# A planned one-core attention and gated-product kernel: two accumulating transfers more per query block, four more up tiles through ScalarE, four batches of value head sums, and nine wide dummy matmuls

## The chip, the cores and the metric

The kernel runs on one core of one Trainium2 chip. The metric is device microseconds of one execution. The kernel before was run three times: 265.95, 266.19 and 266.68 us, median 266.19 us. One more execution, of 266.25 us, was profiled, and the rows quoted in this document are of that one. The engines are called as in the profile: PE (TensorE matmuls), PEld (its weight loads), DVE (VectorE), ACT (ScalarE), POOL (GpSimd) and SP (the engine that issues most transfers).

## The reference

The input x has 2048 rows of 640 columns. Everything is bfloat16 at the ends.

```python
xn = _layernorm(x)
qkv = xn @ wqkv                     # 32 heads of 20, q, k, v
idx = pos[:, None] - 2 * arange(8)  # eight keys per row, two apart, none before row 0
logits = einsum("bhsd,bhswd->bhsw", q, k[idx]) * 20 ** -0.5
o = einsum("bhsw,bhswd->bhsd", softmax(logits), v[idx])
h = (xn' @ w_gate) * (xn' @ w_up)   # 1536 columns
return x + o @ wo + h @ w_down
```

Here xn' is the same normalised x. So there are three kinds of work: dense products with weights (q, k, v, gate, up, down, wo), the eight shifted products of q and k with their head sums, and the eight weighted sums over v.

## The kernel before

**Planner.** The kernel is written as tasks with the tiles that they read and write. A class `Sched` (lines 50 to 351) picks, task by task, the one that could start first on its engine by a table of costs that stands in the code (`occ`, `lat`, and for accumulating transfers `acc` in lines 149 to 153), and writes out one fixed instruction order for each engine with the waits between them. So the costs are used only while the program is written; on the chip each engine runs its list in order, and each instruction waits for what it needs. A change of a cost can reorder everything behind it.

**Tiling.** The 2048 rows are four blocks j of 512. The transposed normalised x is `XNT`; the 640 columns are five chunks c of 128, and the 1536 columns of gate and up are twelve tiles m of 128. PSUM has eight banks of 512 columns.

**Dense work on PE.** `proj_group`, `proj_v` and `q_bank` make q, k and v (lines 698 and 730). `gu` (line 1287) goes through pairs (j, m) in the order of `SEQ` (line 1277): five matmuls of 512 columns with a gate tile, then five with an up tile (line 1314). ACT copies the gate result out of PSUM (line 703). The up result is multiplied in by DVE straight from PSUM (line 1323), unless the pair is in `FAST` (line 1467): then ACT copies the up tile too, into one of two tiles `UF` (`fev`, line 1357), and DVE multiplies two bfloat16 tiles (line 1361). `dn` and `dn_piece` (lines 1387 and 1400) add up twelve matmuls with w_down and five with wo for each piece of 128 rows and 320 columns (line 1416); for blocks 0 to 2 the result leaves through ACT into `FB0` and an accumulating transfer `oadd` into the output (line 1442).

**Logits.** For blocks 0 and 1 DVE makes products of q and k for four shifts at once (`narrow`, line 880), and PE adds up heads with a matrix of ones (line 1012). For blocks 2 and 3 chunks 0 to 3 are made by `wide`, two shifts at once, in fp32, straight from the PSUM bank of q (line 929, tiles `PRF`), and are added on POOL before PE sees them. For each block, each half r of the shifts and each pair of shifts q0 there are four chunk products and one product of the fifth chunk, so four additions:

- `sum32` with p = 0 adds chunk 1 to chunk 0 (name `qsum{j}_{r}_{q0}_0`); for (r, q0) in `BY_DMA[0]` by an accumulating transfer in SBUF that POOL issues (line 951), else by a POOL add (line 955);
- the same call then adds the fifth chunk (name with `c` at its end, line 966; line 962 if (r, q0) is in `LAST_DMA`, which is empty);
- `close` calls `sum32` with p = 1, again by transfer or by add;
- `qend{j}_{r}_{q0}` is the last add, always on POOL (line 988).

Blocks 2 and 3 are joined: PE sums their heads (line 1012) in one group of sixteen matmuls when all eight `qend` are done. PE's list is in order, so it stands still there if they are late. Softmax of blocks 2 and 3 comes behind it.

**Values.** `weighted` and `unit` (lines 1134 and 1151) take twenty units u, five for each block: DVE multiplies v by the weights (line 1191) into one of three tiles `PV`, POOL adds the two halves (line 1196) into `SV`, two adds for each unit, and PE sums heads with four small matmuls for each unit (line 1250) in batches that end with the units in `BATCH` (line 1105): five, five, five, three and two units. Each unit of a batch needs a PSUM bank; ACT copies it out into `OT` (line 1259), which the wo matmuls read.

**Start.** `warm(18)` (line 1495) makes PE multiply zeros before any input has landed.

Of the kernel before, what the change touches and what calls it, by code (L numbers as in the profile page):

```python
# [15 lines left out]
NF = 12  # L16
# [5 lines left out]
TS = 128  # L22
JB = 512
HB = 1024
QB = 256
# [24 lines left out]
class Sched:  # L50
# [78 lines left out]
    def op(self, eng, fn, r=(), w=(), dma=False, name="", occ=None, lat=None, lock=False, nbytes=0, mode=0, group=None, extra=0.0, acc=0.0, land=None):  # L129
        X = _Op()  # L130
        X.eng, X.fn, X.name, X.dma, X.group = eng, fn, name, dma, group
        X.needs_tick, X.event, X.pre_know, X.idx = False, None, None, len(self.ops)
        X.nth = self.n_eng[eng]
        self.n_eng[eng] += 1
        rk = [k for a in r for k in self.keys(a)]
        wk = [k for a in w for k in self.keys(a)]
        deps = self.deps_of(eng, rk, wk)
        if lock:
            deps.update({d.idx: d for d in self.port["pool" if eng == "dve" else "dve"]})
        if occ is None and not dma:  # L140
            occ = 0.1
        inorder = eng in ("pe", "act", "dve")
        start = max([self.t[eng]] + [d.end for d in deps.values()])
        if lock:
            start = max(start, self.t_lock)
        if eng == "pe" and mode != self.pe_mode:
            start += 0.1
            self.pe_mode = mode
        if dma:
            self.t[eng] = start + (0.48 if occ is None else occ)  # L150
            if acc:
                self.t_acc = max(self.t_acc, start + 3.8) + acc
                X.end = self.t_acc
            else:
                self.t_data = max(self.t_data, start + 1.2) + nbytes / 280e3
                X.end = self.t_data + 0.8 + extra
            if land is not None:
                X.end, self.t_data = land, max(land - 0.8, self.t_data - nbytes / 280e3)
        else:
            self.t[eng] = start + occ  # L160
            X.end = start + (occ if lat is None else lat)
        if lock:
            self.t_lock = start + occ
        last = {}
        keep = []
        for d in deps.values():
            if d.dma or d.eng == "pool":
                keep.append(d)
            else:
                b = last.get(d.eng)  # L170
                if b is None or b.idx < d.idx:
                    last[d.eng] = d
        X.deps = keep + list(last.values())
        for d in X.deps:
            if not d.dma:
                d.needs_tick = True
        for k in rk:
            st = self.state.get(k)
            if st is None:
                self.state[k] = [None, [X]]  # L180
            elif inorder and st[1] and st[1][-1].eng == eng and not st[1][-1].dma:
                st[1][-1] = X
            else:
                st[1].append(X)
        for k in wk:
            self.state[k] = [X, []]
        if dma:
            if group is None or group not in self.groups:
                sem = self.nc.alloc_semaphore(f"dma{self.n_dma}")
                self.n_dma += 1  # L190
                if group is not None:
                    self.groups[group] = [sem, []]
            if group is None:
                X.event = (sem, 16)
            else:
                g = self.groups[group]
                g[1].append(X)
                X.event = (g[0], 16)
        if lock:
            self.port[eng] = [X] if eng == "dve" else self.port[eng] + [X]  # L200
            if eng == "dve":
                self.port["pool"] = []
        self.ops.append(X)
        return X
# [151 lines left out]
def build_kernel(nc, A_x, A_wqkv, A_wo, B_x, B_w_gate, B_w_up, B_w_down, out):  # L356
    K = Sched(nc)
    op = K.op
# [63 lines left out]
    PRD += [sb("PRD12", [128, 4, JB], at=a_sc), sb("PRD13", [128, 4, JB], at=a_sc + 4096)]  # L422
    PRD32 = [K.sbuf(f"PRF{i}", [128, 2, JB], FP32, K.base[p.name]) for i, p in enumerate(PRD)]
    QUAD = {2: (1, 0), 3: (1, 0)}
    LAST_DMA = ()
    BY_DMA = (((0, 0), (0, 2)), ((1, 0), (1, 2)))
    a_xr = place[0]
    FB0 = sb("FB0", [128, 5, D])
# [12 lines left out]
    ZERO = sb("ZERO", [128, JB])  # L441
# [235 lines left out]
            yield Task("sp", dmat, r=[xs], prio=1)  # L677
        mark("xnt", t)

    def warm(n):  # L680
        for _ in range(n):
            op("pe", lambda e: e.matmul(PS[:, 7, 0:QB], ZERO[:, 0:128], ZERO[:, 0:QB], start=True, stop=True),
               r=[ZERO[:]], w=[PS[:, 7, :]], name="warm", occ=0.2 if n > 3 else 0.12)

    def wcols(which, c, m):
        if which == 2:
# [77 lines left out]
    def proj_qk():  # L764
        for pair in (0, 2):
            for which in (0, 1):
                for t in (pair, pair + 1):
                    yield have("xnt", t)
                    K.spawn(proj_group([(which, 0, 4 if pair else 5)], t * TS, TS, 10 if pair else FIRST + 0.5 * which + 0.2 * t, None))
            if pair:  # L770
                for which in (0, 1):
                    K.spawn(proj_group([(which, 4, 1)], pair * TS, 2 * TS, 10.2, None))
        for t in (4, 6):
            yield have("xnt", t + 1)
            for items in ([(0, 0, 2)], [(1, 0, 2)], [(0, 2, 2)], [(1, 2, 2)], [(0, 4, 1), (1, 4, 1)]):
                K.spawn(proj_group(items, t * TS, 2 * TS, 11 + t * 0.1, None))
        for j in (2, 3):
            yield have("xnt", 4 * j + 3)
            for m in range(NCH):
                for which in (0, 1):  # L780
                    if which or j not in QUAD or m == NCH - 1:
                        K.spawn(proj_group([(which, m, 1)], j * JB, JB, 12 + j, None))
# [61 lines left out]

    def products():
        rows = {j: [] for j in range(NJ)}
        joined = []
        holds = {}
        for at, (j, kind) in enumerate(ORDER):
            if kind == "w":  # L850
                if j not in holds:
                    yield from fetch(j, 0, holds.setdefault(j, {c: [] for c in range(4)}))
                yield from wide(j, rows[j], holds[j])
            else:
                if len(QUAD.get(j, ())) == 2 and j not in holds and (j, "w") == ORDER[at + 1]:
                    yield from fetch(j, 0, holds.setdefault(j, {c: [] for c in range(4)}))
                for r in (1, 0):
                    for c in range(NCH - 1 if r in QUAD.get(j, ()) else 0, NCH):
                        yield from narrow(j, r, c, rows[j])
            if len(rows[j]) == 10 - 4 * len(QUAD.get(j, ())) and kind == ("w" if j in QUAD else "n"):  # L860
                if j in JOIN:
                    joined.append((j, rows[j]))
                    if len(joined) == len(JOIN):
                        K.spawn(logits(*joined))
                else:
                    K.spawn(logits((j, rows[j])))
        mark("products")

    def narrow(j, r, c, slots):
# [40 lines left out]
    def wide(j, slots, hold):  # L910
        halves = [(r, q0) for r in QUAD[j] for q0 in (0, 2)]
        acc, parts = {}, {1: [], 0: []}
        lastc = {r: [n, 0] for n, _, r in slots}
        slots.clear()
        for c0 in (0, 2):
            for i, (r, q0) in enumerate(halves):
                f = []
# [29 lines left out]
    def sum32(j, r, q0, p, a, b, last=None):  # L947
        x, y = PRD32[a][:], PRD32[b][:]
        name = f"qsum{j}_{r}_{q0}_{p}"
        if (r, q0) in BY_DMA[p]:  # L950
            yield Task("pool", lambda: op("pool", lambda e: e.dma_start(x, y, accum_op=ALU.add), r=[x, y], w=[x], dma=True,
                                          name=name, occ=0.88, acc=3.4), r=[x, y], w=[x], prio=4)
        else:
            yield calm
            yield Task("pool", lambda: op("pool", lambda e: e.tensor_tensor(x, x, y, ALU.add), r=[x, y] + tokens(), w=[x],  # L955
                                          name=name, occ=2.36, lock=True), r=[x, y], w=[x], prio=5, lock=True)
# [3 lines left out]
        z = PRD[last[0]][:, q0:q0 + 2, :]  # L960
        if (r, q0) in LAST_DMA:
            yield Task("pool", lambda: op("pool", lambda e: e.dma_start(x, z, accum_op=ALU.add), r=[x, z], w=[x], dma=True,
                                          name=name + "c", occ=0.88, acc=3.4), r=[x, z], w=[x], prio=4)
        else:
            yield calm
            yield Task("pool", lambda: op("pool", lambda e: e.tensor_tensor(x, x, z, ALU.add), r=[x, z] + tokens(), w=[x],  # L966
# [135 lines left out]
        yield Task("sp", move, r=[L[:]], prio=4)  # L1102

    NU = NJ * NCH
    BATCH = (4, 9, 14, 17, 19)

    def vx_loads():
        yield have("products")
# [291 lines left out]
    def dn_piece(j, t, nb, rows, c0, c1):  # L1400
# [38 lines left out]
        def add_out():  # L1439
            d = ohbm[j * JB:(j + 1) * JB, :].rearrange("(t p) n -> p t n", p=128)  # L1440
            f = F[:, 0:4, :]
            stores.append(op("pool", lambda e: e.dma_start(d, f, accum_op=ALU.add), r=[f, ("outx",)], w=[("out", j)], dma=True,
                             name=f"oadd{j}", occ=0.88, acc=4))

        def store():
            if t == NT - 1:
# [17 lines left out]
        yield Task("pe", down, prio=41, banks=1, keep=0 if count.get(("ot", j), 0) >= NCH else next_sums, r=[WD[:], WO[:]])  # L1464
        K.spawn(tail())

    FAST = [(1, m) for m in range(6, NF)] + [(2, m) for m in range(4, 8)]
    JOIN = (2, 3)
    SLIP = 0.3
    N_PE_T = 4  # L1470
    BN_AFTER = (4,)
# [20 lines left out]
    x_load(2, land=9.0)  # L1492
    wqkv_load(1, 3, NCH, land=10.0)
    K.t["act"] = 2.1
    warm(18)

    def misc():
        yield have("xnt", NT - 1)
# [61 lines left out]
```

## Time and profile before

| what | value |
|---|---|
| three runs | 265.95, 266.19, 266.68 us; median 266.19 |
| profiled execution | 266.25 us, of it 264.4 us from the first to the last instruction |
| PE busy | 259.8 us (98%) |
| DVE busy | 220.1 us (83%) |
| POOL busy | 160.8 us (61%) |
| ACT busy | 111.9 us (42%) |
| DMA queues' share of the 16 engines | 44.3% for SP's loads and stores, 13.5% for POOL's accumulating transfers |

The profile has several views. The page gives sums and the chain of work that ended last, followed back from the end. The chain can also be asked for in order of time, piece by piece. The timeline lists merged instructions with the idle time before them, and windows give busy times of each engine in chosen stretches. The view of one line gives how long its transfers took from issue to landing. A row of merged instructions begins with the start and the busy time in us.

### The profile page before, as it was taken

To read this page: it belongs to the slowest core of one execution; us is meant where nothing else is said; L and a number is where in the kernel's file an instruction comes from. 1 tells how busy PE (TensorE), PEld (TensorE's weight loads), DVE (VectorE), ACT (ScalarE), POOL (GpSimd) and SP (SyncE) were. 2 spreads that over 40 slices of the span, in tenths; PEclk is the share of its full clock that TensorE was granted. 3 is DMA by queue.
4 is the path that set the end of the run, shared out by engine and by line. 5 is a ranking of instruction groups with operands and counts; after the bars stand their busy time and mean duration, and the time that the engine had idled before them with its cause. 6 is when DMAs were issued, how large, how long until landed. Compare 5 with 4: busy or idle time off the path is not lost.

```text
span 264.4 us, 4405 instructions
## 1 busy us (share of the span) xinstructions
PE 259.8 (98%) x1748; PEld 151.8 (57%) x1748; DVE 220.1 (83%) x259; ACT 111.9 (42%) x203; POOL 160.8 (61%) x97
## 2 busy tenths in 40 slices
PE   7999999999999999999999999999999999999996
PEld 4896975444444444444444444477646775776675
DVE  4787899999998799778779999999899998995032
ACT  3468987556612221224268652531235134213100
POOL 3000000000599998899973575599999999999300
DMA  6964679960379995470249425736586537600711
GB/s 207 373 211 84 126 95 383 443 233 18 121 136 187 234 222 111 85 144 1 61 132 308 90 47 121 152 86 157 153 166 138 147 93 124 129 1 0 102 50 50
DMA packets 39685, 37.83 MB, mean 143 GB/s; under 512 B 15697, under 2 KB 37329, under 8 KB 39633
## 3 DMA queue, kind: packets, MB, share of 16 engines
q1 hardware_dynamic: 36688, 31.32, 44.3%
q0 software_dynamic: 2736, 6.16, 13.5%
q8 instruction: 13, 0.21, 0.4%
q10 hardware_dynamic: 240, 0.07, 0.1%
q14 instruction: 8, 0.06, 0.1%
HBM read 25.07 MB, written 7.23 MB: 122 GB/s over the span
## 4 chain that ended last, share of the span: by engine, by line
PE 96%; DMA 2%; DVE 1%; SPq 0%; ACT 0%; issue 0%
PE PS L1314 39%; PE PS L1416 28%; PE PS L698 23%; PE PS L1012 2%; PE PS L1250 2%; PE PS L730 2%; DMA XST<-in_A_x_dram 2%; DVE STATS L574 0%; PE PS L642 0%; SPq L480 0%; ACT XNT L655 0%; DVE XNS L603 0%; ACT SD L584 0%; DVE FB L1429 0%; DVE MV L577 0%
## 5 line engine op out<-in xcount | busy, mean ns | idle before, releaser
L1196 POOL TENSOR_TENSOR SV<-PV 128x1024 bf16<-128x1024 f32 x40 | 94.4, 2384 | 17.1 <-DVE PV L1191 5.9
L1191 DVE TENSOR_TENSOR PV<-VX,PS 128x1024 f32<-128x1024 bf16 (+1 forms) x54 | 90.8, 1730 | 1.5 <-POOL SV L1196 1.5
L698 PE MATMUL PS<-XNT,WQKV 128*128 128x512 bf16 (+2 forms) x390 | 60.8, 316 | 0.0
L1314 PE MATMUL PS<-XNT,WG 128*128 128x512 bf16 x240 | 59.7, 379 | 0.0
L1314 PE MATMUL PS<-XNT,WU 128*128 128x512 bf16 x240 | 59.6, 379 | 0.0
L698 PEld LDWEIGHTS PS<-XNT,WQKV 128*128 128x128 bf16 x390 | 37.9, 112 | 21.9 <-ACT LOG L1023 0.8
L1314 PEld LDWEIGHTS PS<-XNT,WG 128*128 128x128 bf16 x240 | 23.2, 98 | 28.9 <-DVE XNT L1323 0.8
L1314 PEld LDWEIGHTS PS<-XNT,WU 128*128 128x128 bf16 x240 | 23.5, 98 | 28.0
L929 DVE TENSOR_TENSOR PRF<-PS,KT 128x1024 f32<-128x1024 f32 x32 | 37.9, 1218 | 0.3 <-PE PS L698 0.3
L955 POOL TENSOR_TENSOR PRF<-PRF,PRF 128x1024 f32<-128x1024 f32 x8 | 22.0, 2755 | 20.6 <-DVE LOG L1072 20.6
L703 ACT ACTIVATE HT<-PS 128x512 bf16<-128x512 f32 x24 | 14.3, 597 | 34.5 <-PE PS L1314 34.5
L1416 PE MATMUL PS<-WD,HT 128*128 128x320 bf16 x192 | 28.7, 299 | 0.0
L703 ACT ACTIVATE FB<-PS 128x320 bf16<-128x320 f32 x24 | 10.5, 437 | 40.4 <-PE PS L1416 40.4
L880 DVE TENSOR_TENSOR PRD<-QT,KT 128x2048 bf16<-128x2048 bf16 x24 | 27.3, 1222 | 0.0
L1031 POOL MEMSET LOG<- 32x6 bf16 (+6 forms) x7 | 0.4, 95 | 44.2 <-ACT LOG L1023 44.2
L1416 PE MATMUL PS<-WO,OT 128*128 128x320 bf16 (+2 forms) x165 | 26.5, 295 | 0.0
L1416 PEld LDWEIGHTS PS<-WD,HT 128*128 128x128 bf16 x192 | 18.8, 98 | 7.6
L988 POOL TENSOR_TENSOR PRD<-PRF,PRF 128x1024 bf16<-128x1024 f32 x8 | 21.5, 2768 | 0.1
L966 POOL TENSOR_TENSOR PRF<-PRF,PRD 128x1024 f32<-128x1024 f32 x8 | 19.5, 2543 | 0.0
L1416 PEld LDWEIGHTS PS<-WO,OT 128*128 128x128 bf16 x165 | 16.0, 98 | 5.8
L1323 DVE TENSOR_TENSOR HT<-HT,PS 128x512 bf16<-128x512 bf16 x18 | 12.3, 686 | 7.0 <-PE PS L1314 7.0
L1429 DVE TENSOR_TENSOR FB<-PS,XR 128x320 bf16<-128x320 f32 (+2 forms) x9 | 4.1, 454 | 16.5 <-PE PS L1416 16.5
(72 smaller groups left out, 247.1 us busy)
## 6 DMA issues: line engine op xcount, KB each, us to landing
VX<-v_scratch SPq DMA_DIRECT2D x80, 130.0 KB, 3.1
PRF<-PRF POOLq DMA_DIRECT2D x8, 512.0 KB, 5.1
XST<-in_A_x_dram SPq DMA_DIRECT2D x16, 160.0 KB, 5.4
v_scratch<-VST SPq DMA_DIRECT2D x4, 640.0 KB, 6.5
WG<-in_B_w_gate_dram SPq DMA_DIRECT2D x1, 1920.0 KB, 8.8
WU<-in_B_w_up_dram SPq DMA_DIRECT2D x1, 1920.0 KB, 12.2
out_dram<-in_A_x_dram SPq DMA_DIRECT2D x1, 1920.0 KB, 19.7
WD<-in_B_w_down_dram SPq DMA_DIRECT2D x1, 1920.0 KB, 8.2
```

Source lines behind the costliest of these rows:

```text
L698: op("pe", (lambda o, l, x, c, first: lambda e: e.matmul(o, l, x, start=first, stop=(c == NCH - 1)))(o, l, x, c, first), r=[l, x], w=[o], ...
L703: X = op("act", (lambda o, i: lambda e: e.activation(o, i, ACT.Copy))(o, i), r=[i], w=[o], name=name, occ=0.12 + n * 0.9e-3)
L880: op("dve", lambda e: e.tensor_tensor(s[:], qb, kv, ALU.mult), r=[q, rk], w=[s[:]], name=f"prod{j}_{r}_{c}", occ=1.15, lock=True)
L929: X = op("dve", lambda e: e.tensor_tensor(o[:], qb, kv, ALU.mult), r=[q, rk, ("qev", j, c)], w=[o[:]], name=f"prow{j}_{r}_{c}_{q0}", occ=1.17)
L955: yield Task("pool", lambda: op("pool", lambda e: e.tensor_tensor(x, x, y, ALU.add), r=[x, y] + tokens(), w=[x], name=name, occ=2.36, lock ...
L966: yield Task("pool", lambda: op("pool", lambda e: e.tensor_tensor(x, x, z, ALU.add), r=[x, z] + tokens(), w=[x], name=name + "c", occ=2.36 ...
L988: yield Task("pool", lambda: op("pool", lambda e: e.tensor_tensor(o, a, y, ALU.add), r=[a, y] + tokens(), w=[o], name=f"qend{j}_{r}_{q0}", ...
L1191: last[0] = op("dve", lambda e: e.tensor_tensor(p, vw, a, ALU.mult), r=[vv] + rk, w=[p], name=f"pv{u}_{x}_{r0}", occ=0.09 + 1.1 * nr)
L1196: X = op("pool", lambda e: e.tensor_tensor(o, p[:, :, 0, :], p[:, :, 1, :], ALU.add), r=[p[:]] + tokens(), w=[o], name=f"pva{u}_{x}", occ= ...
L1314: op("pe", (lambda l, x, c: lambda e: e.matmul(PS[:, b, :], l, x, start=(c == 0), stop=(c == NCH - 1)))(l, x, c), r=[l, x], w=[PS[:, b, :] ...
L1323: X = op("dve", lambda e: e.tensor_tensor(h, h, PS[:, hold[1], :], ALU.mult), r=[h, PS[:, hold[1], :]], w=[h], name=f"h{m}_{j}", occ=0.65)
L1416: op("pe", (lambda l, x, i: lambda e: e.matmul(dst, l, x, start=(i == 0), stop=(i == n - 1)))(l, x, i), r=[l, x], w=[PS[:, b, :]], name=f" ...
```

## The change

Five things are changed in the code:

1. `LAST_DMA` holds (1, 2) and (0, 2). For blocks 2 and 3 that makes four of the eight additions of the fifth chunk accumulating transfers instead of POOL adds.
2. `FAST` gets (3, 0) to (3, 3): four more up tiles are copied by ACT and multiplied by DVE from SBUF.
3. `BATCH` is (4, 9, 14, 19): five units in each of four batches; units 15 to 19 are one batch.
4. `warm(9, JB)`: nine dummy matmuls of 512 columns instead of eighteen of 256.
5. The costs with which the planner counts are changed: an accumulating transfer between tiles from 3.8 + 3.4 to 1.6 + 3.1, an accumulating store of the output from 3.8 + 4 to 1.6 + 4.6.

The rest (`products`, `wide`, the shape of `JOIN`) makes the code more general and gives the same tasks with the settings that stand in this kernel.

```diff
-                self.t_acc = max(self.t_acc, start + 3.8) + acc
+                self.t_acc = max(self.t_acc, start + 1.6) + acc
...
-    LAST_DMA = ()
+    LAST_DMA = ((1, 2), (0, 2))
...
-    def warm(n):
+    def warm(n, cols=QB):
         for _ in range(n):
-            op("pe", lambda e: e.matmul(PS[:, 7, 0:QB], ZERO[:, 0:128], ZERO[:, 0:QB], start=True, stop=True),
-               r=[ZERO[:]], w=[PS[:, 7, :]], name="warm", occ=0.2 if n > 3 else 0.12)
+            op("pe", lambda e: e.matmul(PS[:, 7, 0:cols], ZERO[:, 0:128], ZERO[:, 0:cols], start=True, stop=True),
+               r=[ZERO[:]], w=[PS[:, 7, :]], name="warm", occ=0.4 if cols > QB else 0.12)
...
-                                          name=name, occ=0.88, acc=3.4), r=[x, y], w=[x], prio=4)
+                                          name=name, occ=0.88, acc=3.1), r=[x, y], w=[x], prio=4)
...
-                                          name=name + "c", occ=0.88, acc=3.4), r=[x, z], w=[x], prio=4)
+                                          name=name + "c", occ=0.88, acc=3.1), r=[x, z], w=[x], prio=4)
...
-    BATCH = (4, 9, 14, 17, 19)
+    BATCH = (4, 9, 14, 19)
...
-                             name=f"oadd{j}", occ=0.88, acc=4))
+                             name=f"oadd{j}", occ=0.88, acc=4.6))
...
-    FAST = [(1, m) for m in range(6, NF)] + [(2, m) for m in range(4, 8)]
-    JOIN = (2, 3)
+    FAST = [(1, m) for m in range(6, NF)] + [(2, m) for m in range(4, 8)] + [(3, m) for m in range(4)]
+    JOIN = ((2, 3),)
...
-    warm(18)
+    warm(9, JB)
```

What the planner makes of it can be read from the two instruction lists, which carry no times. PE's list is the same up to the gate and up pairs of block 0. There one group of ten q matmuls stands a pair earlier. The head sums of the logits of blocks 2 and 3 stand two pairs of gate and up earlier, and so does the first batch of value head sums; the second stands three and a half pairs earlier, the third three. The last batch, now of five units, stands ahead of the last pair of block 3 and of all of block 3's w_down and wo matmuls; before, its three and two units stood behind the last pair, with 36 w_down matmuls between them.

On POOL the order of blocks 2 and 3 is, with T for a transfer: `qsum2_1_0_0`, `qsum2_1_2_0`, T `qsum2_0_0_0`, T `qsum2_1_2_0c`, T `qsum2_0_2_0`, `qsum2_1_0_0c`, T `qsum2_1_0_1`, `qsum2_0_0_0c`, T `qsum2_1_2_1`, `qsum2_0_0_1`, T `qsum2_0_2_0c`, `qend2_0_0`, `qend2_1_0`, `qend2_1_2`, `qsum3_1_0_0`, `qsum2_0_2_1`, `qsum3_1_0_0c`, T `qsum3_0_0_0`, `qend2_0_2`, T `qsum3_0_2_0`, `qsum3_1_2_0`, T `qsum3_1_2_0c`, `qsum3_0_0_0c`, T `qsum3_0_2_0c`, T `qsum3_1_0_1`, T `qsum3_1_2_1`, `qsum3_0_0_1`, `qend3_0_0`, `qsum3_0_2_1`, `qend3_1_0`, `qend3_0_2`, `qend3_1_2`. The four transfers whose names end with `c` read a bfloat16 tile (`PRD`) and add it to an fp32 tile; the eight others have fp32 on both sides.

On DVE, from unit 4 on the up products of block 3 stand elsewhere: those of (3, 0) to (3, 2), now the short form, come together in the middle of unit 5's products, that of (3, 3) in unit 9's, and (3, 4) and (3, 5) in unit 10's; before, all six stood among the products of units 4 and 5. On ACT there are four copies more. SP's list differs in the place of one unit's four loads of v.

More of the change, by code (lines that the diff above doesn't have):

```diff
@@ L775, in proj_qk @@
             for items in ([(0, 0, 2)], [(1, 0, 2)], [(0, 2, 2)], [(1, 2, 2)], [(0, 4, 1), (1, 4, 1)]):
-                K.spawn(proj_group(items, t * TS, 2 * TS, 11 + t * 0.1, None))
+                if 1 not in QUAD or items[0][0] or items[0][1] == 4:
+                    K.spawn(proj_group(items, t * TS, 2 * TS, 11 + t * 0.1, None))
         for j in (2, 3):
@@ L846, in products @@
         rows = {j: [] for j in range(NJ)}
-        joined = []
+        joined = {}
         holds = {}
@@ L857, in products @@
                 for r in (1, 0):
+                    if (r in QUAD.get(j, (r,) if kind == "n" else ())) != (kind == "n"):
+                        continue
                     for c in range(NCH - 1 if r in QUAD.get(j, ()) else 0, NCH):
                         yield from narrow(j, r, c, rows[j])
[L860 to L866, printed above, removed]
+            if len(rows[j]) == 10 - 4 * len(QUAD.get(j, ())) and kind == ("n" if j not in QUAD else "w" if len(QUAD[j]) > 1 else "m"):
+                group = next((g for g in JOIN if j in g), (j,))
+                joined[group] = joined.get(group, ()) + ((j, rows[j]),)
+                if len(joined[group]) == len(group):
+                    K.spawn(logits(*joined[group]))
         mark("products")
@@ L912, in wide @@
         acc, parts = {}, {1: [], 0: []}
-        lastc = {r: [n, 0] for n, _, r in slots}
-        slots.clear()
+        lastc = {r: [n, 0] for n, _, r in slots if r in QUAD[j]}
+        slots[:] = [e for e in slots if e[2] not in QUAD[j]]
         for c0 in (0, 2):
```

## Prediction

> **What bounds the kernel now.** I read four views, from the whole to the place. The page first: PE is busy 98% of the span, and the chain that ended last is 96% PE.
>
> ```profile
> span 264.4 us, 4405 instructions
> ...
> PE 259.8 (98%) x1748; PEld 151.8 (57%) x1748; DVE 220.1 (83%) x259; ACT 111.9 (42%) x203; POOL 160.8 (61%) x97
> ...
> PE 96%; DMA 2%; DVE 1%; SPq 0%; ACT 0%; issue 0%
> ```
>
> A busy PE need not be a full one, so the chain in order of time comes next. The end of it:
>
> ```profile
> 101.84 32.38 PE PS L1314 x150
> 134.22 0.98 PE PS L1012 x16
> ...
> 223.52 18.58 PE PS L1416 x136
> 242.10 0.76 PE PS L1250 x12
> 242.86 5.00 PE PS L1416 x36
> 247.86 0.55 PE PS L1250 x8
> 248.40 13.75 PE PS L1416 x117
> 262.15 0.02 issue
> ```
>
> Here 150 matmuls of 512 columns take 32.38 us, 0.216 us each; the same 0.216 us holds for every gate and up block of the chain. Nothing but PE stands in it from 11.7 us to 262.15 us. PE doesn't wait there, so no other engine can give time back; each can only take some, by making PE wait.
>
> What the reader is to see in the head sums is a fixed cost. Twenty small matmuls take 1.19 us, twelve 0.76, eight 0.55: 0.053 us each and 0.12 us for the batch. The work behind a batch pays too: 36 w_down matmuls took 5.00 us, where 136 of them at full pace take 18.47 us, so 36 would take 4.89: 0.11 us more. A batch costs 0.23 us beside its matmuls.
>
> The timeline shows the start and POOL:
>
> ```profile
> 1.27 3.46 PE L682 MATMUL PS<-ZERO 128*128 128x256 bf16 x18 [1.27 <-DVE ZERO L482]
> 5.42 0.63 PE L642 MATMUL PS<-IDENT,XNS 128*128 128x128 bf16 x5 [0.70 <-DVE XNS L603]
> ...
> 69.11 4.67 POOL L955 TENSOR_TENSOR PRF<-PRF,PRF 128x1024 f32<-128x1024 f32 x2 [20.65 <-DVE LOG L1072]
> 73.72 1.03 POOL L951 DMA_DIRECT2D PRF<-PRF  x1
> 74.48 2.45 POOL L966 TENSOR_TENSOR PRF<-PRF,PRD 128x1024 f32<-128x1024 f32 x1
> ...
> 171.84 21.07 POOL L1196 TENSOR_TENSOR SV<-PV 128x1024 bf16<-128x1024 f32 x9 [2.73 <-DVE PV L1191]
> ```
>
> PE is done with its dummies 0.70 us before it can start the first real matmul, which waits for DVE. A POOL add is followed by the next after 2.31 us (nine in 21.07 us with overlap; 69.11 to 73.72 for two); a transfer holds POOL 0.6 to 0.8 us.
>
> **The change, part by part.**
>
> *Four batches.* Sums of the same twenty units, one batch less: 0.23 us off PE's path. This is the only PE work that the change removes.
>
> *Nine dummies.* 9 x 512 are as many columns as 18 x 256. The eighteen took 3.46 us; at the pace of the first twelve (2.53 us by a window, 0.211 us for 256 columns) all nine would take 3.8 us and end at 5.07, still ahead of 5.42. Cost 0 as long as they are under 4.15 us. Below, nothing is to be gained: the next thing waits for DVE.
>
> *Four fifth-chunk adds become transfers.* POOL loses 4 x 2.31 = 9.2 us of adds and gets 4 x 0.65 = 2.6 us of issuing. That is off the path; what counts is when the last `qend3` is done, since PE's heads of blocks 2 and 3 wait for it. In the new order PE comes to them two pairs earlier: 134.15 (first L1012 in the timeline) - 2 x 2.16 = 129.8, and to block 3's eight matmuls at 130.3. In the old order POOL's last `qend` (127.42, two in 5.18) ended at 132.6, 1.5 us before PE.
>
> POOL's new end is a sum over its list. Needed are the transfers' landings. By the view of line 951, asked for each transfer by itself, the eight took 5.2, 5.7, 7.5, 6.1, 4.5, 4.9, 4.6 and 5.0 us from issue. So one alone takes 4.5 to 5.2, and the next lands 3.25 to 3.45 us after it when they queue (issued at 73.72, 76.55, 78.10, 82.83, landed at 78.97, 82.2, 85.65, 88.9). With 3.3 us between landings the six of block 2 land at 79.0, 82.3, 85.6, 88.9, 92.2 and 95.5. `qend2_1_2` needs the fifth and starts at 92.2 instead of 94.8; behind it stand three adds, 94.5 to 101.4 (the second needs 95.5: no wait). Then the list of block 3: transfer 101.4, landing 106.1; add to 104.4; transfer, landing 109.4; add to 107.3; transfer, landing 112.7; add to 110.3; three transfers (the last needs DVE's product, that ended at 113.1 before), landing 116.0, 119.3, 122.6. Six adds from 113.4 are each ready in turn (`qend3_1_2` needs 122.6 and starts at 125): 127.3, and 0.45 us until its end is seen, **127.7**. If DVE's last products of block 3 come no sooner than their own waits in the old order allow, I get 129.2. PE needs it at 130.3: margin 1.1 to 2.6 us, cost 0.
>
> *What the trace doesn't show* is a transfer that adds bfloat16 to fp32, as these four do. Bounds from the nearest rows: the output's accumulating transfers, bfloat16 on both sides, land 640 KB in 7.0 us (line 1442), 11 ns for each KB against 9 to 10 of the fp32 ones, so bfloat16 alone makes a transfer neither much faster nor slower; were it faster, the path would gain nothing, as PE has no wait to lose. From above the longest landing of all, 7.5 us, which as a spacing would be 4.2 us more each. I take 3.3, since the destination (fp32, 512 KB) is that of the rows. With e us more for each of the four, the fifth landing of block 2 moves by e, block 3's last by about 3e; it passes 130.3 at e = 1.6. At e = 3.3 the sum gives 138.5, that is 8 us of wait.
>
> *Four up tiles through ACT.* ACT gets 4 x 0.60 us, DVE loses 4 x (0.69 - 0.42) = 1.1 us. The cover is ACT's idle time (1.56 us between copies at 158 to 165 us). But the copy of (3, 2) waits for the multiplication of (3, 0) to free its `UF` tile, and the next pair's bank waits for the copies behind: three copies, 1.6 us by rows of 0.49 us steps. PE is there at 166.6 (old place less 4.3), so the multiplication must end by 165.0. In the old order unit 5's second half ended at 171.8 on DVE; less six direct products that no longer stand before it (3.6 us) and 3.3 to 4.3 us for the earlier start, 163.9 to 164.9, and 0.4 for the multiplication: 164.3 to 165.3. PE waits 0 to 0.3 us; I take 0, with little room.
>
> *The last batch* stands 20.8 us before PE's end (pair and switch 2.27, 102 and 51 matmuls 18.5): PE comes to its last unit at 240.9. POOL's adds run on without a stop from unit 5 (171.84) to the last (246.83), 75.0 us, of which 0.8 was an output transfer that now stands behind. Started 6.9 us or more earlier, they end at 239.1 or before. Margin 1.8 us, cost 0. Behind the batch, ACT's five copies delay the last gate copy to 243.4 and its product to 244.1; PE needs it at 244.9.
>
> **Sum**: 266.25 (264.4 of span and 1.85 around it, which stays) - 0.23 = 266.02, say **266.0 us**; the profiled execution is 0.06 above the median of the runs, so the median would be 265.96.
>
> **A rule beside a row.** The landings above are 4.5 to 5.2 us alone and 3.3 us apart for 512 KB. The Trainium skill, "DMA: Bandwidth & Descriptors", section "Anatomy of one DMA — SWDGE (gpsimd) path", fits 2.0 us plus the bytes over 436 GB/s; as an estimate that is 3.2 us alone and 1.2 us apart. By the rule the transfers would never queue, POOL would end by its adds alone, and PE's sum would be the same. The row shows accumulating transfers at less than half that rate, and decides.
>
> **Rivals.**
> - *Slow transfers (slower).* The queue of six transfers becomes what PE's heads wait for: from about 3.85 us between landings (3.45 is the longest seen), or from e = 1.6 for the four mixed ones. For it: twelve transfers of 3.3 us are 40 us in a stretch of 54, the unseen form, four in flight at times where three were seen, and SP's loads of v in the same stretch. Against: landings 3.25 us apart while SP loaded too. Price: 4.0 us apart gives the last `qend3` at 132.3, PE 2.0 us late, 268.0; e = 3.3 gives 274.
> - *The `UF` tile (slower).* DVE's handshakes with POOL run 1 us later than counted; PE waits before the block behind the first batch. Price 1.0, so 267.0; 0.3 would still be no change, 266.3.
> - *Nothing of it counts.* The saved switch is lost in a wait of 0.2 us, as at the last gate copy: 266.25.
> - *Faster than counted.* It would need PE work that isn't in the chain; the only waits of PE are before 8.7 us, some 1.5 us in all, behind input transfers and DVE that the change leaves alone. 265.2 at most.
>
> **How the numbers follow.** Forecast with no wait over 0.3 us, the lost switch included: 0.70. Slow transfers 0.18, `UF` tile 0.07, faster 0.05. A difference under 0.3% (0.8 us) is about what a measurement of this kernel can't tell from none. The forecast and its small waits lie within it: same 0.70 + 0.01 of the rivals' small ends; slower 0.24; faster 0.05. The forecast's own range is 265.6 to 266.7 (the three runs lie 0.7 apart). The range reaches from 265.5 to 268.0, to the first price of slow transfers; beyond lie some 0.1 and, below, 0.04.
>
> **What would show it.** Right: one L1250 batch less, PE without idle time from 8.7 us on, first L1012 of blocks 2 and 3 near 129.8, the last `qend` ending before 130. Wrong: PE idle before L1012 with POOL as releaser and landings of line 963 over 5 us behind each other; or PE idle at 166 behind ACT.

## The result: 267.56 us, 0.5% slower, and the profile after

The changed kernel takes 267.56 us (median of eight runs, 266.84 to 268.11); the kernel before takes 266.18 us (eight runs, 265.73 to 266.68). The ratio is 1.0051, with a 95% interval of 1.0034 to 1.0069. The prediction was 266.0 us and no measurable change. The time stands inside the range, but on the slower side, and the runs spread over 1.27 us where those of before spread over 0.95. The profiled execution of after took 266.84 us, the least of the eight, so it shows the smaller form of what went wrong.

Its page first: span, busy times, and the engines' shares of the chain.

```profile
span 265.1 us, 4367 instructions
...
PE 259.6 (98%) x1722; PEld 150.8 (57%) x1739; DVE 218.8 (83%) x259; ACT 113.3 (43%) x207; POOL 155.9 (59%) x97
...
PE 90%; ACT 6%; DMA 1%; issue 1%; DVE 1%; SPq 0%
```

POOL has lost 4.9 us, DVE 1.3 us, and the span has still grown by 0.7. ACT now has a share of the chain, so PE may wait somewhere. Most of that share (13.7 us) lies before 35.4 us and costs nothing: PE's first head sums start at 45.02 us, in before at 45.19. The chain in order of time shows the rest at the first batch of value head sums (line 1251; the columns are start, length, what):

```profile
164.10 1.24 PE PS L1315 x5
165.34 0.56 PE PS L1251 x8
165.90 0.33 ACT UF L703
166.23 0.14 issue
166.37 0.59 ACT XNT L703
166.96 0.50 ACT ZERO L703
```

The timeline of PE shows the stop itself (a row is start, length, engine, line, operation; in brackets the idle time before it and who ended it):

```profile
165.27 0.83 PE L1251 MATMUL PS<-SV,SEL 128*32 128x512 bf16 x12
166.53 0.89 PE L1251 MATMUL PS<-SV,SEL 128*32 128x512 bf16 x8 [0.43 <-ACT UF L703]
```

The batch of twenty stops after twelve (the chain counts only eight of them), because the banks of its last two units are freed by ACT's copies of the pairs (3, 2) and (3, 3), and these are late. From the starts of the matmuls the batch costs 2.33 us between its neighbours; a batch of twenty that waits for nothing costs 1.29. PE loses 1.04 us here. What ACT waited for is seen in the timelines of ACT and DVE:

```profile
165.88 0.60 ACT L703 ACTIVATE UF<-PS 128x512 bf16<-128x512 f32 x1 [2.96 <-PE PS L1251]
```

```profile
163.10 2.35 DVE L1192 TENSOR_TENSOR PV<-VX,PS 128x1024 f32<-128x1024 bf16 x2 [0.21 <-POOL SV L1197]
165.42 0.43 DVE L1362 TENSOR_TENSOR XNT<-XNT,UF 128x512 bf16<-128x512 bf16 x1
```

The copy into `UF` starts when DVE's product of (3, 0), which reads the old content of that tile, ends at 165.85; the row's releaser names PE, whose result had long been there. The prediction wanted that product done by 165.0. It is the place of the rival "the `UF` tile". But why is DVE late? Looking back over DVE's timeline from 165 to 70 us, its longest wait is for a transfer; in before, no wait of DVE from 70 to 130 us ended with one:

```profile
103.93 0.69 DVE L1324 TENSOR_TENSOR HT<-HT,PS 128x512 bf16<-128x512 bf16 x1 [0.66 <-PE PS L1315]
107.20 1.23 DVE L930 TENSOR_TENSOR PRF<-PS,KT 128x1024 f32<-128x1024 f32 x1 [2.58 <-DMA PRF<-PRF]
```

DVE stood 2.58 us before it could overwrite a tile `PRF`, since the first transfer of block 3 (`qsum3_0_0_0`) still read it. That transfer was issued at 100.71 and landed at 107.17, 6.46 us; in before the same one took 4.51 us (100.89 to 105.40), and DVE did not wait. The view of the DMA queues says what lay beside it. From 100 to 106 us (packets, MB, share of the 16 engines), before and then after:

```profile
q0 software_dynamic: 175, 0.65, 57.2%
q1 hardware_dynamic: 27, 0.02, 1.5%
```

```profile
q1 hardware_dynamic: 782, 0.71, 62.1%
q0 software_dynamic: 138, 0.54, 45.5%
```

q0 holds POOL's transfers, q1 SP's. In before SP's loads of v for units 0 to 3 had landed by 101.26; in after the last lands at 105.27 and they share the engines with the transfer. And why they are late stands in the same view from 74 to 95 us, before and then after:

```profile
q0 software_dynamic: 576, 2.10, 54.2%
q1 hardware_dynamic: 3417, 2.11, 44.8%
```

```profile
q0 software_dynamic: 864, 3.15, 73.6%
q1 hardware_dynamic: 2396, 1.26, 25.9%
```

The shares add to 99% in both. The 16 engines were full already before the change. With the two extra transfers of block 2 (1.05 MB more in q0), 0.85 MB of SP's loads moved behind 95 us, at some 0.21 MB for each us four us of work. Most of the delay is already in SP's issues: the last of these loads is issued at 98.77 us, in before at 95.42. Whether the full engines held SP up, or something else about POOL's transfers, no run separates.

How does a wait at 107 us reach 165 us? DVE itself does not stay late. The rows of POOL and then of DVE in after:

```profile
113.90 0.86 POOL L952 DMA_DIRECT2D PRF<-PRF  x1 [1.67 <-DVE PRF L930]
128.88 4.67 POOL L1197 TENSOR_TENSOR SV<-PV 128x1024 bf16<-128x1024 f32 x2
```

```profile
127.67 0.69 DVE L1324 TENSOR_TENSOR OT<-OT,PS 128x512 bf16<-128x512 bf16 x1 [0.96 <-PE PS L1315]
131.26 2.29 DVE L1192 TENSOR_TENSOR PV<-VX,PS 128x2048 f32<-128x2048 bf16 x1 [0.75 <-POOL SV L1197]
```

POOL waits 1.67 us for the late DVE before block 3's last transfer, and runs almost without a stop from there to its first value adds. DVE has caught up by 127.67, where it waits for PE. At 131.26 it waits 0.75 us until POOL's add frees a tile `PV`, and is late again, now up to the `UF` tile. The run with held loads (a_vxheld, below) has the same rows without the lateness.

Theory V says so: block 2's extra transfers delay the loads of v, these delay block 3's first transfer, that holds DVE, DVE holds POOL, POOL holds DVE again, and PE pays at the first place without slack. Its rivals: theory U, that the tiles `UF` cost by themselves; theory S, that the nine wide dummies make the start uneven; theory T, that the accumulating transfers are late or slow by themselves.

### The profile page after: what moved, and what is told of

It reads as the page before. It is cut to its first block, busy times and chain, and to the rows that moved or that the text cites. A ratio compares the mean times of both kernels' runs of the same rounds, so it can differ in the third digit from the quotient of the medians.

```text
span 265.1 us, 4367 instructions
## 1 busy us (share of the span) xinstructions
PE 259.6 (98%) x1722; PEld 150.8 (57%) x1739; DVE 218.8 (83%) x259; ACT 113.3 (43%) x207; POOL 155.9 (59%) x97
## 4 chain that ended last, share of the span: by engine, by line
PE 90%; ACT 6%; DMA 1%; issue 1%; DVE 1%; SPq 0%
PE PS L1315 39%; PE PS L1417 28%; PE PS L698 17%; ACT XNS L609 3%; PE PS L1013 2%; PE PS L730 2%; PE PS L1251 2%; DMA XST<-in_A_x_dram 1%; ACT QT L703 1%; ACT VST L703 1%; ACT KT L703 1%; ACT SD L584 0%; DVE STATS L574 0%; PE PS L642 0%; SPq L480 0%
## 5 line engine op out<-in xcount | busy, mean ns | idle before, releaser
L1315 PE MATMUL PS<-XNT,WG 128*128 128x512 bf16 x230 | 57.5, 379 | 0.4
L956 POOL TENSOR_TENSOR PRF<-PRF,PRF 128x1024 f32<-128x1024 f32 x8 | 19.3, 2428 | 20.8 <-DVE LOG L1073 20.7
L1417 PE MATMUL PS<-WO,OT 128*128 128x320 bf16 (+2 forms) x165 | 27.1, 295 | 0.0
L989 POOL TENSOR_TENSOR PRD<-PRF,PRF 128x1024 bf16<-128x1024 f32 x8 | 19.0, 2392 | 0.2
L574 DVE BATCH_NORM_STATS2 STATS<-XST 128x6 f32<-128x320 bf16 x32 | 14.1, 471 | 2.1 <-DMA XST<-in_A_x_dram 2.1
```

Of the source, the lines that this page charges most:

```text
L574: op("dve", lambda e: e.bn_stats(o, a), r=[a], w=[("st", t, i)], name=f"bn{t}_{i}", occ=0.49)
L1315: op("pe", (lambda l, x, c: lambda e: e.matmul(PS[:, b, :], l, x, start=(c == 0), stop=(c == NCH - 1)))(l, x, c), r=[l, x], w=[PS[:, b, :] ...
L1417: op("pe", (lambda l, x, i: lambda e: e.matmul(dst, l, x, start=(i == 0), stop=(i == n - 1)))(l, x, i), r=[l, x], w=[PS[:, b, :]], name=f" ...
```

## The experiments

Labels with `a_` are the changed kernel with one thing altered, those with `b_` the kernel before, those with `h_` the changed kernel with loads held back. Medians are of 6 to 12 runs, not all on one chip; each ratio is to the runs of the kernel before of the same chip, with its 95% interval. "PE's wait" is the time of the first batch of value head sums beyond 1.29 us, from the starts of the matmuls (less 0.216 us where the record of a matmul is missing).

| kernel | median us | last load of v lands | first transfer of block 3 takes | DVE waits for it | PE's wait |
|---|---|---|---|---|---|
| before | 266.18 | 101.3 | 4.51 | 0 | 0 |
| after | 267.56 | 105.3 | 6.46 | 2.58 | 1.04 |
| a_warm18 | 267.85 | 105.4 | 6.63 | 2.75 | 1.21 |
| a_uf3 | 267.36 | 105.7 | 7.31 | 3.42 | 1.24 |
| a_c_only2 | 267.37 | 105.2 | 7.67 | 3.79 | 1.80 |
| a_fast_off | 268.50 | 105.9 | 7.63 | 3.74 | 2.17 |
| a_c_only3 | 266.00 | 102.1 | 5.50 | 1.19 | 0.23 |
| a_c_adds | 265.70 | 102.0 | 5.88 | 1.57 | 0 |
| a_vxheld | 265.86 | 100.1 | 4.56 | 0.67 | 0.05 |

**A third tile for the copies (a_uf3).**

```diff
-    NUF = 2
+    NUF = 3
-    UF = [sb("UF0", ...), ZERO]
+    UF = [sb("UF0", ...), ZERO, UX[:, 0, :]]
```

> The changed kernel with a third tile for the up copies (the unused tile UX takes the place of a wait), all else as it is. Theory U (the copy of (3, 2) waits for the product of (3, 0), and PE waits 1.04 us for the copies behind it at 165.7 us): PE runs through there, and the median falls from 267.56 us by 1.04 to about 266.5; if the spread of the runs (266.84 to 268.11) comes from the same place, to 265.9 with a spread of 0.7 as before. Theory S (the nine wide dummies make the start uneven): the profiled wait may go, but the runs stay spread over more than 1 us. Theory T (the accumulating transfers make POOL and DVE late in some executions): median 266.5 or more and a wide spread.

Measured: 267.36 us, ratio 1.0046 (1.0029 to 1.0063), 266.43 to 268.33. The copy no longer waits for the tile, and no gain is seen. The chain of this kernel shows what has taken its place, POOL's add of unit 4:

```profile
164.09 2.38 POOL SV L1197
166.47 0.04 issue
166.52 0.39 PE PS L1251 x2
```

The batch needs that add, the add stands behind DVE's products, and those are late too (DVE waits 3.42 us at 108 here). But the planner has also put the batch five matmuls earlier, at 164.40 us instead of 165.27, so it needs the add sooner than after did, where the add ended at 165.38. So this run speaks against theory U and does not decide it; the next run and the held loads do.

**The old list of copied up tiles (a_fast_off).**

```diff
-    FAST = [(1, m) for m in range(6, NF)] + [(2, m) for m in range(4, 8)] + [(3, m) for m in range(4)]
+    FAST = [(1, m) for m in range(6, NF)] + [(2, m) for m in range(4, 8)]
```

> The changed kernel with the old list FAST, so the up tiles of (3, 0) to (3, 3) are multiplied straight from PSUM again; the planner moves 13 DVE instructions. Theory U: no copy waits for a tile, the 1.04 us wait of PE at 165.7 is gone, 266.0 to 266.5. DVE has 1.1 us more to do; were DVE so late that the direct products hold PE's banks instead, 266.8 or more. Theories S and T: about 267.5 still.

Measured: 268.50 us, ratio 1.0090 (1.0059 to 1.0121), slower than the changed kernel and up to 270.34. The chain:

```profile
165.80 0.82 PE PS L1251 x12
166.61 0.01 issue
166.62 0.68 DVE XNT L1324
167.30 1.13 DVE PV L1192
168.43 0.61 DVE XNT L1324
```

With DVE late, the direct products hold PE's banks. So the loss is there without the four copies, and they do not make it. That they made it smaller is what the medians say; the intervals of the two ratios overlap a little.

**The dummies, both ways (a_warm18, b_warm9).**

```diff
-    warm(9, JB)
+    warm(18)
```

> The changed kernel with eighteen dummies of 256 columns again; no other instruction moves. Theory U and T: 267.5, with the same spread of more than 1 us. Theory S (nine wide dummies cost time or make the start uneven): 266.3 to 266.8 with a spread under 0.8.

> The kernel before with nine dummies of 512 columns; no other instruction moves. Theories U and T: as the kernel before, 266.2, within 0.3. Theory S: 266.8 to 267.5, and a spread of more than 1 us.

Measured: 267.85 us for the changed kernel with eighteen short dummies (1.0062, 1.0044 to 1.0081; 266.93 to 268.57), and 265.86 us for the kernel before with nine wide ones (0.9997, 0.9988 to 1.0005; 265.78 to 266.38). No other instruction moves in either. The dummies change nothing that these runs can see, and theory S falls.

**Loads held back (a_vxheld).** The loads of v for units 2 and 3, eight of the sixteen early ones, get one more dependency, on block 3's last add. The lists of all engines stay the same, so this takes their traffic out of 95 to 105 us and puts it behind 128 us.

```diff
+    HELD = (2, 3)
...
-                rk = [("vscr", "pad")] + ...
+                rk = ([("qend", 3, 1, 2)] if u in HELD else []) + [("vscr", "pad")] + ...
```

> The changed kernel, but the loads of v for units 2 and 3 wait for the last add of block 3's logits (eight of the sixteen early loads, which ran from 95 to 105 us beside the transfers); no instruction moves on any engine's list. Theory V (block 2's two extra transfers push the loads of v back from 101.3 to 105.3 us, the first transfer of block 3 stands behind them and lands 6.46 us after its issue instead of 4.51, DVE waits 2.58 us for the tile that it reads and stays that late until PE waits at 165.7 us): the first transfer of block 3 lands under 5 us after issue, DVE's wait falls under 1 us, PE's first batch of value head sums costs 1.3 us instead of 2.33, the median is 266.0 with a spread under 0.8. Theory U (the tiles UF by themselves): 1 us of wait stays at 165.7, median 267 or more. If the loads come too late for unit 2 at 140 us, DVE waits for them there.

Measured: 265.86 us, ratio 0.9984 (0.9970 to 0.9997), twelve runs from 265.57 to 266.34. The view of the transfers' line for the one issued near 100 us, in after and then here (duration of the issue, its place, and the time to landing):

```profile
L952 POOL DMA_DIRECT2D PRF<-PRF x1: 871/871/871, 100.7 to 100.7; - x1
...
DMA to landing us min/median/max: 6.5/6.5/6.5
```

```profile
L952 POOL DMA_DIRECT2D PRF<-PRF x1: 871/871/871, 100.5 to 100.5; - x1
...
DMA to landing us min/median/max: 4.6/4.6/4.6
```

DVE's wait shrinks with it, in its timeline:

```profile
105.08 1.23 DVE L930 TENSOR_TENSOR PRF<-PS,KT 128x1024 f32<-128x1024 f32 x1 [0.67 <-DMA PRF<-PRF]
```

And the first batch runs through, in the chain:

```profile
163.89 1.24 PE PS L1320 x5
165.13 1.19 PE PS L1256 x20
166.32 1.24 PE PS L1320 x5
```

All twenty matmuls are in one piece. Between DVE's wait and this batch, three of the rows that carried the lateness in after are earlier now:

```profile
112.31 0.86 POOL L952 DMA_DIRECT2D PRF<-PRF  x1 [0.28 <-DVE PRF L930]
127.28 4.69 POOL L1202 TENSOR_TENSOR SV<-PV 128x1024 bf16<-128x1024 f32 x2
```

```profile
130.23 2.28 DVE L1197 TENSOR_TENSOR PV<-VX,PS 128x2048 f32<-128x2048 bf16 x1
```

Up to 100 us PE, DVE and POOL are all 0.21 us earlier in this execution than in after. Beyond that DVE is 1.9 us earlier at its wait (105.08 against 107.20), POOL 1.4 us from its last transfer on, DVE not at all at 127 us (127.46 against 127.67) and 0.8 to 1.0 us from 130 us up to the product of (3, 0). DVE's other wait for a transfer, 0.86 us at 90.64 in after, is still here (0.98 us) and costs nothing.

The copies, the dummies, the batches and all twelve transfers are still there, and the loss is gone. The runs spread over 0.77 us now; that is a weak sign by itself, since the 35 runs of before on this chip reach 267.89. The time and the rows decide for theory V. Theory U falls with it: the two tiles `UF` are used as in after, and were where the lateness came out, not where it came from.

**The transfers in one block only (a_c_only2, a_c_only3).**

```diff
-        if (r, q0) in LAST_DMA:
+        if j == 2 and (r, q0) in LAST_DMA:
```

> The changed kernel with the fifth-chunk adds by transfer in block 2 alone. Theory V: the loads of v end at 105 us again, DVE waits 2 us and more for the first transfer of block 3, and the time is 267 or more. Rival (the mixed transfers of block 3 are what is late): no such wait, 266.2.

> The changed kernel with the fifth-chunk adds by transfer in block 3 alone (two of four). Theory V: block 2's transfers are four as in the kernel before, the loads of v end by 102 us, DVE doesn't wait over 1 us at the first overwritten tile of block 3; 266.0 to 266.4. Rival (any extra transfer makes block 3 late): 267.

Measured: 267.37 us with block 2's (1.0044, 1.0019 to 1.0070), 266.00 us with block 3's (0.9988, 0.9970 to 1.0005). The order on the engines moves too, which is why the held loads are the cleaner test; but the signs are as theory V has them. DVE's timeline with block 2's alone:

```profile
108.20 1.23 DVE L930 TENSOR_TENSOR PRF<-PS,KT 128x1024 f32<-128x1024 f32 x1 [3.79 <-DMA PRF<-PRF]
```

Block 3 has no mixed transfer in that kernel, and still its first one is late. Theory T, that transfers of the new form are late by themselves, falls. Why this one takes 7.7 us where after's took 6.5, with loads that end at the same time, stays open. Five kernels have the same lists up to there but for the dummies (after, a_warm18, a_uf3, a_fast_off and this one), and it took 6.46 to 7.67 us in them; with one trace of each, nothing shows what sets it.

**No fifth-chunk transfer (a_c_adds).**

```diff
-    LAST_DMA = ((1, 2), (0, 2))
+    LAST_DMA = ()
```

> The changed kernel with no fifth-chunk transfer (LAST_DMA empty), with its four batches, four more copied up tiles, costs and dummies. Theory V: the loads of v as before, DVE not late, 266.0, that is a batch less than the kernel before (0.2). Theory U: PE waits for the copies of up tiles, 266.8 or more. Rival: POOL with four adds more is late at the joined heads near 130 us.

Measured: 265.70 us, ratio 0.9977 (0.9962 to 0.9991), the fastest of all. DVE waits 1.57 us for the first transfer, but PE's first batch of value head sums comes 4 us later in this order (169.32 us) and doesn't notice. The runs of before on the same chip have a median of 266.13, so it gains 0.43 us; a batch less explains 0.21 of them (below), and what the rest is stays open.

**The transfers alone (b_ldma).** The kernel before with `LAST_DMA` as in after, with the old costs.

> The kernel before with the four fifth-chunk transfers alone (LAST_DMA; old costs, batches, copies and dummies). Theory V: the loads of v end near 105 us instead of 101.3, the first transfer of block 3 lands over 6 us after its issue, DVE waits over 2 us for it, and PE waits somewhere behind: 267 to 268.5 with a wide spread. Theory U (the copied up tiles are what costs): as the kernel before, 266.2.

Measured: 266.64 us, ratio 1.0019 (1.0004 to 1.0034). A loss, but a smaller one than expected, and by another way. The loads of v do land late (105.6), but in this order POOL comes to block 3's first transfer only at 105.2, when they are nearly through: it takes 4.6 us and DVE doesn't wait. The loss is at the joined heads, in the chain:

```profile
130.37 4.63 POOL PRD L988 x2
135.00 0.14 issue
135.14 0.40 PE PS L1012 x4
```

PE waits some 0.4 us for POOL's last adds. So the loads are delayed by block 2's transfers in either kernel; the collision with block 3's first transfer needs the earlier place that this one has in the changed order (100.71 us).

**Controls on the held loads (b_vxheld, h_batch5, h_fast_off).** The same edit in the kernel before; and in a_vxheld five batches again, or the old list `FAST`.

> The kernel before with the loads of v for units 2 and 3 held back until block 3's last add, nothing else. Theory V: there is no lateness to take away, so no gain: 266.1, within 0.3. Were the loads of v a cost of the kernel before too, it would gain some tenths.

> The changed kernel with the loads held back (265.86) and five batches again. By the fixed cost of a batch (0.21 to 0.23 us) 266.08; PE's batches cost 1.29, 1.29, 1.29, 0.86 and 0.64 us. If the last batches wait for POOL, more.

> The changed kernel with the loads held back (265.86) and without the four more copied up tiles. Theory V: the copies only mattered because DVE was late (without them 268.5 in the changed kernel); with DVE in time the time is 265.9 to 266.2. If the short products are needed to keep DVE in time at all, PE waits at the first batch still, 266.5 or more.

Measured: 266.30 us (0.9998, 0.9986 to 1.0009), 266.07 us (0.9995, 0.9985 to 1.0004) and 266.07 us (0.9992, 0.9981 to 1.0002). Holding loads back is worth nothing where nothing was late. Five batches cost 0.21 us over four, as the fixed price says, and with DVE in time the four more copies are worth as much; both differences lie inside the intervals, and a_vxheld ran on another chip, so the medians alone don't show them.

## Why the prediction was wrong

- *Four batches, −0.23*: right. From the starts of the matmuls an undisturbed batch of twenty costs 1.29 us, one of eight (in h_batch5) 0.64, so 0.21 is fixed; the medians agree (266.07 − 265.86 = 0.21 us) but do not show it by themselves.
- *Nine dummies, 0*: right (b_warm9). They took 4.02 us, where 3.8 were counted and 4.15 allowed.
- *Spacing of the transfers*: right where it was asked. The landings of after are 2.4 to 3.5 us apart within block 2, 1.9 to 2.9 in block 3, with no mixed one over 3.2; the last `qend` ended at 128.9 (127.7 or at worst 129.2 were foreseen), and PE began the joined heads at 129.65 without a wait. The rival "slow transfers" did not come. (Its figure of 138.5 for e = 3.3 does not follow from "about 3e", which gives 122.6 + 9.9 + 2.3 + 0.45 = 135.3, and so 271 and not 274; the forecast does not rest on it.)
- *The failed step* is the cost 0 of these transfers, as the part on the fifth-chunk adds has it. Its "transfer 101.4, landing 106.1" took the 4.5 to 5 us of before, where SP's loads landed by 101.26 and the transfer had the engines to itself; with the loads delayed by block 2's own extra transfers it is 100.71 and 107.17. I had listed "SP's loads of v in the same stretch" as a point for slow transfers and then asked only what they do to the transfers, not what the transfers do to them. And I followed each landing to POOL's next add and to PE, but not to DVE's product that overwrites the transfer's source (line 930). That product waited 2.58 us where the sum has nothing, and the wait went on through POOL and DVE to PE's 1.04 us.
- *The `UF` step*: the demand was right, DVE done by 165.0. The estimate, 164.3 to 165.3, took DVE's earlier start for granted. Without the collision it holds: in a_vxheld the product ends at 164.64, and PE waits 0.05 us. In after it ended at 165.85, and PE idle at 166 behind ACT was one of the prediction's own signs of being wrong. The rival had the right place and the right last link: DVE's handshake with POOL at 131.26 is late. It did not have the source, and it had a chance of 0.07. Its price of 1.0 meets the 1.04 of the profiled execution, the fastest; the median lies 1.6 above the 265.96 of the sum.
- *Luck*: that 267.56 lies in the range is owed to the price of slow transfers, 268.0, which did not come.

The profiled execution adds up: a batch less −0.21, first batch +1.04, third batch +0.05, first projections 0.18 earlier (8.56 against 8.74 us), together +0.70; the span grew from 264.4 to 265.1. That the other runs lose more, up to 1.9 us, fits the table, in which the wait is by and large longer where block 3's first transfer takes longer; the slowest runs have no profile, so for them this is argued and not shown.

A rule would have warned. The row: from 102.5 to 104.0 us of after the trace's packets are 160 KB of POOL's transfer and 154 KB of SP's loads, each about half of the engines' time. The Trainium skill, "DMA: Bandwidth & Descriptors", section "Queues, rings and completion order", says that each DMA engine goes round between the queues that have work, packet by packet. Equal bytes of both queues fit such turns; that they go packet by packet the trace does not show, since its records are 40 of 4096 bytes for POOL and 152 of 1040 bytes for SP. By the rule, what one queue brings more is time taken from the other while the engines are full; here the transfer beside the loads took 6.46 us instead of 4.51.

## What to carry to other kernels

Before work is moved from an engine to DMA, look at the share of the 16 engines in that stretch, not over the whole span (44% and 14% by queue looked like room; from 74 to 95 us it was 99%): here the price of two transfers in a full stretch was paid by the next loads, and by the transfer that then ran beside them. A transfer has two ends: follow its landing to the reader of the result and to the next writer of its source. And where a wait shows up at a small shared tile, compare the rows before it with those of a run that has no such wait: the engine that is late at the tile can have caught up once in between, while another one carried the lateness on.

## What the runs showed of the hardware beyond that

- A transfer in SBUF that adds bfloat16 to fp32 was not dearer than an fp32 one in after: it landed 1.9 to 3.1 us after the one before it, the fp32 ones 2.5 to 3.5 (512 KB written each).
- The issue of a load was slower while POOL's transfers ran: SP's sixteen issues of v in after took 0.43 us in the median, but the first four, from 87.7 to 93.4 us, 1.1 to 1.87 us each; POOL's last transfer of block 2 landed at 93.7. From 94 to 100 us the engines were as full (share 1.10) with SP's own loads, and the issues took 0.43.
